# Second MLP: its first product for pairs of batches by Strassen's scheme, weights and x by way of DRAM

## Chip, cores and metric

One Trainium2 chip, one of its cores. The metric is the device time of one execution in microseconds; less is better. TensorE multiplies, VectorE and ScalarE and GpSimd do the elementwise work, SyncE (SP) issues the DMAs.

## What is computed

Attention over 4 batches x 12 heads (448 positions, 64 wide) with RMS-normalized q and k, then two MLPs over the 1792 rows:

```python
x = attn_out                       # 1792 x 768
h = ((x @ w1) * (x @ w2)) @ w3     # d_ff 1024
x = h @ w_out                      # 1792 x 768
h = x @ w_in                       # 768 x 2048   <- "first product of the second MLP"
g = h * clip(h + 3, 0, 6) / 6
out = g @ w_out2                   # 2048 x 768
```

Weights arrive as 64-bit floats. Every product is taken in three passes: each operand is split into a rounded part (hi) and the rest (lo), and hi*hi, hi*lo and lo*hi are added in one bank.

## The kernel before

Everything is kept transposed: features on the 128 partitions, the 448 positions of one batch (`S`) along the free dimension. One matmul is a 128x128 block of weights against 128x448 of data into one of 8 banks (tags `s`, `t`, `v`, `f`, two banks each).

The attention runs in steps written out by hand; between its instructions `fill` slips in the products of the first MLP (`products`: `layer1(b)`, `layer2(b)` for batches 0 to 3) and, through `prep`, their weights. The first MLP's results go to DRAM (`x2d`) for batches 0 to 2. Those of batch 3 are split straight out of the bank (`L["x2"]`), since the second MLP takes batch 3 first (`order`).

When the attention is over, a loop (L858) issues the rest of the first MLP and, every third step, converts one tile of the second MLP's weights (`conv_w`, `convert`: two passes on ScalarE L137 and L138, two on VectorE L140 and L143). The 32 converted tiles (16 of `win`, 16 of `wo2`, 128x768 each) stay in SBUF as `wf`. The second MLP is the loop L893: for each batch and each of 16 column blocks `m` it splits one tile of `win` and one of `wo2` (`split`: ScalarE copy L851, GpSimd subtraction L852), takes h in 18 matmuls (6 blocks of 128 features x 3 passes, tile `h`), applies the activation (ScalarE L930, VectorE L931), splits g (L934, L935), and takes 18 matmuls of the second product for the step before (`l4_part`, tile `acc`, six banks that collect over all 16 steps). `mm3` (L81 to L83) issues the three passes. Conversions left over are issued among the steps of the first batch. All DMAs go through SP's queue (`dma`, L88).

The order on each engine is set by a planner that takes the program's order as priority and moves ahead what it believes ready; `tc.issue_after` pins an instruction behind another.

## Time and profile before

| what | us |
|---|---|
| median of 3 runs | 1222.15 (1221.26 to 1225.3) |
| span of the profiled execution, first to last instruction | 1219.5 |
| what lies around it, against the median | 2.65 |
| TensorE busy | 1160.4 |
| VectorE, ScalarE, GpSimd busy | 756.6, 726.6, 464.9 |
| second MLP, from 738.2 to the end | 481.3 |

The profile names each group of instructions by line, engine, operation and tile. A matmul's record (0.37 us) overlaps the next one's, so the spacing of starts is what a matmul costs. The busy time of VectorE and GpSimd includes time in which an instruction has begun and is held up. The page gives no time of its own for the profiled execution other than the span.

### The profile page before, as it was taken

Reading aid. Unit: us, or ns where it says so; the run is one execution under the profiler, and the core shown is the slowest. Engines: PE = TensorE matmul, PEld = TensorE weight load, DVE = VectorE, ACT = ScalarE, POOL = GpSimd, SP = SyncE. Lnnn points to the kernel's source line nnn. Section 1 sums busy time; section 2 is a strip of 40 time slices with the busy share of each in tenths; the row PEclk is TensorE's granted clock in tenths of the full one; section 3 lists DMA queues with packets and bytes.
Section 4 is the critical chain, followed back from the end, with each engine's and each line's share of the span. In section 5 each row is a group of like instructions: output and inputs, shape, how many; then the busy total and the mean of one; then the engine's idle time right before and its main releaser. Section 6 shows DMA issues by size and latency. Waiting matters only on the chain.

```text
span 1219.5 us, 16961 instructions
## 1 busy us (share of the span) xinstructions
PE 1160.4 (95%) x5868; PEld 1020.5 (84%) x5868; DVE 756.6 (62%) x1474; ACT 726.6 (60%) x1401; POOL 464.9 (38%) x316
## 2 busy tenths in 40 slices
...
PEclk9799998999999999999999999999999999999999
...
GB/s 277 209 220 239 191 188 196 251 284 293 334 265 254 222 224 249 228 240 197 148 187 360 355 304 207 156 101 23 91 1 1 4 88 1 1 1 46 1 1 46
...
## 3 DMA queue, kind: packets, MB, share of 16 engines
...
q8 instruction: 46, 0.75, 0.3%
...
## 4 chain that ended last, share of the span: by engine, by line
PE 75%; DVE 7%; ACT 5%; DMA 5%; issue 4%; POOL 3%; SPq 0%; ACTq 0%; POOLq 0%; DVEq 0%
PE bank L340 10%; PE acc L81 7%; PE acc L83 7%; PE acc L82 6%; PE h L81 6%; PE h L82 6%; PE h L83 6%; PE bank L345 5%; PE bank L592 4%; PE bank L81 3%; PE bank L82 3%; PE bank L83 3%; DVE PP L573 2%; PE bank L566 2%; PE bank L567 2%
## 5 line engine op out<-in xcount | busy, mean ns | idle before, releaser
L852 POOL TENSOR_TENSOR wis<-wf,wis 128x768 fp32r<-128x768 f32 x63 | 120.0, 1904 | 220.0 <-ACT wis L851 219.9
L340 PE MATMUL bank<-xhl,ws 128*128 128x448 f32 x768 | 184.9, 372 | 2.5 <-ACT bs L316 2.4
L931 DVE SCALAR_TENSOR_TENSOR u<-u,h 128x448 f32<-128x448 f32 x64 | 39.5, 618 | 210.6 <-ACT u L930 210.6
L340 PEld LDWEIGHTS bank<-xhl,ws 128*128 128x128 f32 x768 | 145.1, 191 | 16.5 <-ACT bs L316 3.1
L852 POOL TENSOR_TENSOR wos<-wf,wos 128x768 fp32r<-128x768 f32 x64 | 121.4, 1896 | 91.0 <-ACT wos L851 91.0
L585 ACT ACTIVATE PP<-PP,mx 112x448 f32<-112x448 f32 x192 | 127.2, 664 | 45.0 <-DVE mx L580 36.4
L573 DVE CUSTOM_DVE_ANT_0 PP<-bank,rb,rq 112x448 f32<-112x448 f32 x192 | 129.0, 675 | 34.8 <-PE bank L567 23.9
L83 PE MATMUL acc<-g,wos 128*128 128x448 f32 x384 | 141.3, 368 | 0.0
L82 PE MATMUL acc<-g,wos 128*128 128x448 f32 x384 | 141.3, 368 | 0.0
L81 PE MATMUL acc<-g,wos 128*128 128x448 f32 x384 | 140.0, 368 | 0.0
L81 PE MATMUL h<-x2h,wis 128*128 128x448 f32 x378 | 139.2, 368 | 0.5 <-DVE u L931 0.4
L82 PE MATMUL h<-x2h,wis 128*128 128x448 f32 x378 | 138.9, 367 | 0.0
L83 PE MATMUL h<-x2h,wis 128*128 128x448 f32 x378 | 137.4, 364 | 1.3 <-POOL wis L852 1.3
L930 ACT ACTIVATE u<-h,half 128x448 f32<-128x448 f32 x64 | 40.7, 636 | 156.0 <-PE h L83 156.0
L935 DVE TENSOR_TENSOR g<-u,g 128x448 fp32r<-128x448 f32 x64 | 105.2, 1645 | 37.5 <-ACT g L934 37.5
L851 ACT ACTIVATE wos<-wf 128x768 fp32r<-128x768 f32 x64 | 54.2, 847 | 85.9 <-PE acc L83 85.7
L601 ACT ACTIVATE xh<-bank 128x448 fp32r<-128x448 f32 (+1 forms) x156 | 83.0, 539 | 32.6 <-PE bank L592 29.4
L566 PE MATMUL bank<-K,Q 128*112 128x448 f32 x192 | 76.7, 400 | 25.6 <-DVE mx L573 13.1
L611 DVE TENSOR_TENSOR xl<-bank,xh 128x448 fp32r<-128x448 f32 x142 | 87.3, 616 | 21.9 <-ACT xh L601 20.6
L592 PE MATMUL bank<-ident,PP 112*128 112x112 f32 x672 | 94.4, 264 | 6.0 <-DVE xl L611 5.2
L592 PEld LDWEIGHTS bank<-ident,PP 112*128 112x128 f32 x672 | 77.7, 142 | 26.8 <-issue 6.8
L345 PE MATMUL bank<-xhl,ws 128*128 128x448 f32 x384 | 95.4, 367 | 0.0
...
## 6 DMA issues: line engine op xcount, KB each, us to landing
...
```

The costliest lines, as they stand in the source:

```text
L81: nc.tensor.matmul(ps, lh, rh, start=first, stop=False)
L82: nc.tensor.matmul(ps, lh, rl, start=False, stop=False)
L83: return nc.tensor.matmul(ps, ll, rh, start=False, stop=last)
L340: nc.tensor.matmul(ps[:, :S], w[:, 0, ks], x[:, y, :], start=k == 0 and y == 0, stop=False)
L345: nc.tensor.matmul(ps[:, :S], w[:, 1, ks], L["xhl"][i][:, 0, :], start=False, stop=k == KD - 1)
L566: nc.tensor.matmul(ps[:CP, :S], qs, k1[:, j, :], start=True, stop=False)
L573: anchors[8 * i + s].append(nc.vector.tensor_tensor_reduce(out=T["PP", i][:, c, sl], in0=ps[:CP, :S], in1=T["rb", i][:, sl], op0=ALU.mult, ...
L585: anchors[8 * i + s].append(nc.scalar.activation(v, v, AF.Exp, bias=T["m", i][:, 8 + s : 9 + s], accum_out=T["sum", i][:, s : s + 1]))
L592: nc.tensor.transpose(ps[:, c * CP : c * CP + CP], src[:, c, kb * P : kb * P + P], ident[:CP, :CP])
L611: nc.vector.tensor_sub(lo, ps, hi)
L852: nc.gpsimd.tensor_sub(t[:, 1, :], wf[q], t[:, 0, :])
L935: nc.vector.tensor_sub(g[:, 1, :], u, g[:, 0, :])]
```

## The change

The batches are taken in pairs (0, 1) and (2, 3), and the column blocks of `win` in pairs. With the 6 feature blocks cut into two halves of 3, h of a pair of batches and a pair of column blocks is a 2x2 by 2x2 block product. It is taken in 7 block products of 3 x 3 matmuls (P1 to P7, Strassen's scheme in Winograd's form) where 8 stood. Sums of weight blocks (S1 to S4, VectorE, `prepare`) and of x blocks (T1 to T4, VectorE, `xprep`, `xrest`) are made ahead. The sums of the products are made partly by adding on in a bank (P1+P6+P7+P4 in one, P5+P3 in the other) and partly on VectorE from copies that ScalarE takes of a bank between (`snap`). Only two banks (`sA`, `sB`) serve the products; they change roles after each P4.

The second product of the pair's first batch (`L0` to `L3`) is issued between the products; that of the second batch (kind `M`) follows when all 16 column blocks are done, from g's unsplit form kept in SBUF (`G`). Splits of weights are made for half tiles of 384 columns, the subtraction in turn on VectorE and GpSimd (`halves`).

The 32 converted tiles no longer stay in SBUF: a ring of 12 buffers holds them, each is written to DRAM (`wfd`) at its first release and read back for each later use. All of x passes through `x2d`. The operands of the first pair are built once the last batch's `layer1` is issued, those 22 and T4 of it at the beginning of the second MLP, those of the second pair during the first pair's `M`. The pool of the first MLP is cut in two so that one part is freed ahead of the last `layer2`.

The core of the diff (at the last hunk the removed lines are those from L802 to L944, and the loading, indexing and output code is left out):

```diff
@@ -54,7 +55,8 @@
     rkd = dpool.tile([NP, 2 * S], F32, name="rkd")
     rsd = dpool.tile([NP, 2, S], F32, name="rsd")
     w12d = dpool.tile([M1, 2, P, 2 * DM], F32, name="w12d")
-    x2d = dpool.tile([B - 1, KD, P, S], F32, name="x2d")
+    x2d = dpool.tile([B, KD, P, S], F32, name="x2d")
+    wfd = dpool.tile([2 * M2, P, DM], F32, name="wfd")
     wpd = dpool.tile([KD * M1 // 6, P, 6, 2 * P], F32, name="wpd")
 
     cpool = ctx.enter_context(tc.tile_pool(name="consts", bufs=1, side="left"))
@@ -152,6 +154,9 @@
         yield from wprime()
         for b in range(B):
             yield from layer1(b)
+            if b == B - 1:
+                L["xm"].__exit__(None, None, None)
+                L["half"] = True
             yield from layer2(b)
 
     W = {}
@@ -260,6 +265,8 @@
     def open_l1():
         L["cm"] = tc.tile_pool(name="l1", bufs=1, side="right", **RW)
         pool = L["cm"].__enter__()
+        L["xm"] = tc.tile_pool(name="l1x", bufs=1, side="right", **RW)
+        L["xp"] = L["xm"].__enter__()
         raw, ws = defaultdict(list), {}
         L.update(ws=ws, xhl={}, abh={}, cur=0, pool=pool)
         pieces = [(u, h) for u in range(2, 2 * M1) for h in range(2)]
@@ -268,7 +275,7 @@
         def load():
             if pieces:
                 u, h = pieces.pop()
-                raw[u].append(fetch(pool, w12[u // 2, 1 - u % 2][:, h * NH : h * NH + NH], NH, "raw", 4))
+                raw[u].append(fetch(L["xp"], w12[u // 2, 1 - u % 2][:, h * NH : h * NH + NH], NH, "raw", 4))
 
         def item(u):
 
@@ -303,7 +310,7 @@
             prep[0].step()
 
     def xsplit(i):
-        d = L["pool"].tile([P, 2, S], F32R, tag="xhl", bufs=XB, name="xhl")
+        d = L["xp"].tile([P, 2, S], F32R, tag="xhl", bufs=XB, name="xhl")
         xs = xs_ready.pop(i)
         nc.scalar.activation(d[:, 0, :], xs, AF.Copy)
         nc.gpsimd.tensor_sub(d[:, 1, :], xs, d[:, 0, :])
@@ -357,12 +364,9 @@
         pool = L["pool"]
 
         def evac(n, ps):
-            if b < B - 1:
-                st = pool.tile([P, S], F32, tag="bs", bufs=2, name="bs")
-                nc.scalar.activation(st, ps[:, :S], AF.Copy)
-                dma(x2d[b, n], st)
-            else:
-                L["x2"](n, ps)
+            st = pool.tile([P, S], F32, tag="bs", bufs=2, name="bs")
+            nc.scalar.activation(st, ps[:, :S], AF.Copy)
+            dma(x2d[b, n], st)
 
         for n in range(KD):
             ps = bank("f")
@@ -799,148 +803,310 @@
-...
+    NWF, NWT, AHEAD2 = 12, 8, 6
+    PAIRS = ((0, 1), (2, 3))
...
+    uses = []
+    for p in range(2):
+        for j in range(M2 // 2):
+            uses += [("in", 2 * j), ("in", 2 * j + 1)]
+            if j:
+                uses += [("out", 2 * j - 2), ("out", 2 * j - 1)]
+        uses += [("out", M2 - 2), ("out", M2 - 1)]
+        uses += [("out", q) for q in range(M2)]
...
+    def units():
+        n = 0
+        for v, (kind, q) in enumerate(uses):
+            while v >= used[0] + NWF:
+                yield None
+            t = mp.tile([P, DM], F32, tag="wf", bufs=NWF, name="wf")
+            if v in fresh:
+                r = wr.pop(v)
+                if r.dtype == F32:
+                    nc.gpsimd.tensor_copy(t, r)
+                    yield 0.9
+                else:
+                    yield from convert(t.bitcast(I32), r)
+                n += 1
+                load_raw(n + 1)
+                yield 0.0
+            else:
+                dma(t, wfd[q + (M2 if kind == "out" else 0)])
+                yield 0.0
+            wf[v] = t
+    unit = units()
...
+    def drop(v):
+        kind, q = uses[v]
+        t = wf.pop(v)
+        used[0] += 1
+        if v in fresh:
+            dma(wfd[q + (M2 if kind == "out" else 0)], t)
...
+    def halves(t, src):
+        nc.scalar.activation(t[:, 0, :], src, AF.Copy)
+        nsplit[0] += 1
+        (nc.vector if nsplit[0] % 2 else nc.gpsimd).tensor_sub(t[:, 1, :], src, t[:, 0, :])
         return t
 
+    def xprep(p):
+        b1, b2 = PAIRS[p]
+        for k in range(KD // 2):
+            x = {}
+            for z, b, n in (("11", b1, k), ("21", b1, k + 3), ("12", b2, k), ("22", b2, k + 3)):
+                x[z] = utile()
+                dma(x[z], x2d[b, n])
+            t1, t2 = utile(), utile()
+            nc.vector.tensor_sub(t1, x["12"], x["11"])
+            nc.vector.tensor_sub(t2, x["22"], t1)
+            for z, src in (("11", x["11"]), ("21", x["21"]), ("T2", t2), ("T1", t1)):
+                xo[z, k] = halves(xtile(z, k), src)
+                yield 1.2
+            nc.vector.tensor_sub(x["12"], x["22"], x["12"])
+            xo["T3", k] = halves(xtile("T3", k), x["12"])
+            yield 1.8
+    def xrest(p):
+        x = []
+        for k in range(KD // 2):
+            x.append(utile())
+            dma(x[k], x2d[PAIRS[p][1], k + 3])
+        for k in range(KD // 2):
+            xo["22", k] = halves(xtile("22", k), x[k])
+            yield 1.2
+            d = utile()
+            nc.vector.tensor_sub(d, xo["21", k][:, 0, :], xo["T2", k][:, 0, :])
+            nc.vector.tensor_sub(x[k], xo["21", k][:, 1, :], xo["T2", k][:, 1, :])
+            nc.vector.tensor_add(d, d, x[k])
+            xo["T4", k] = halves(xtile("T4", k), d)
+            yield 1.8
+    ORDER = ("P1", "P2", "P6", "L0", "L1", "P5", "P7", "L2", "L3", "P3", "P4")
+    RIGHT = {"P1": "11", "P2": "21", "P6": "T2", "P5": "T1", "P7": "T3", "P3": "22", "P4": "T4"}
...
+    def prepare(i):
+        kind, p, j, v, h = items[i]
+        if kind[0] != "P":
+            upto(v)
+            t = mp.tile([P, 2, NH], F32R, tag="wt", bufs=NWT, name="wt")
+            wt[i] = halves(t, wf[v][:, h * NH : h * NH + NH])
+            if h:
+                drop(v)
+            return
+        upto(v[1])
+        a11, a12 = wf[v[0]][:, :NH], wf[v[0]][:, NH:]
+        a21, a22 = wf[v[1]][:, :NH], wf[v[1]][:, NH:]
+        def temp(z, x, y, op):
+            sx[z] = mp.tile([P, NH], F32, tag="sx", bufs=3, name="sx")
+            nc.vector.tensor_tensor(out=sx[z], in0=x, in1=y, op=op)
+            return sx[z]
+        if kind == "P6":
+            temp("S1", a21, a22, ALU.add)
+            temp("S2", sx["S1"], a11, ALU.subtract)
+        src = dict(P1=a11, P2=a12, P4=a22).get(kind)
+        if src is None:
+            if kind == "P7":
+                src = temp("S3", a11, a21, ALU.subtract)
+            elif kind == "P3":
+                src = temp("S4", a12, sx["S2"], ALU.subtract)
+            else:
+                src = sx["S2" if kind == "P6" else "S1"]
+        t = mp.tile([P, 2, NH], F32R, tag="wt", bufs=NWT, name="wt")
+        wt[i] = halves(t, src)
+        if h:
+            drop(v[0])
+            drop(v[1])
...
+        if now[0] % 2 and "half" not in L:
+            spend(1.5)
+        if "half" in L:
+            if xg is None:
+                xo["cm"] = tc.tile_pool(name="xl", bufs=1, side="left", **RW)
+                xo["pool", True] = d1.enter_context(xo["cm"])
+                xg = xprep(0)
+            for _ in range(2):
+                if next(xg, None) is None:
+                    prep_to(ready[0] + 1 if ready[0] < AHEAD2 else 0)
+    for _ in xg:
+        pass
...
+    def finish(p, j, z, src):
+        b, q = (z % 10 - 1), 2 * j + z // 10 - 1
+        if b == 0:
+            _, u = nonlinear(src, None)
+            gsplit(p, 0, q, u)
+            return
+        if (p, j) not in G:
+            G[p, j] = rp.tile([P, 2, S], F32, tag="G", bufs=M2 // 2, name="G")
+        nonlinear(src, G[p, j][:, q % 2])
+    sA, sB = bank("s", "sA"), bank("s", "sB")
+    swap = [(sA, sB)]
+    snap = {}
+    def product(kind, i, ps, first):
+        w = wt.pop(i)
+        z = RIGHT[kind]
+        for k in range(KD // 2):
+            ks = slice(k * P, k * P + P)
+            x = xo[z, k]
+            for n, (a, c) in enumerate(((0, 0), (0, 1), (1, 0))):
+                nc.tensor.matmul(ps[:, :S], w[:, a, ks], x[:, c, :], start=first and k == 0 and n == 0,
+                                 stop=k == KD // 2 - 1 and n == 2, skip_group_check=not first)
+    def strassen(i):
+        kind, p, j, _, _ = items[i]
+        a, c = swap[0]
+        own = c if kind in ("P2", "P5", "P3") else a
+        product(kind, i, own, kind in ("P1", "P2", "P5"))
+        r = own[:, :S]
+        if kind in ("P1", "P6", "P5"):
+            snap[kind] = utile()
+            nc.scalar.activation(snap[kind], r, AF.Copy)
+            return
+        if kind == "P4":
+            finish(p, j, 21, r)
+            swap[0] = (c, a)
+            return
+        s, z = {"P2": ("P1", 11), "P7": ("P5", 22), "P3": ("P6", 12)}[kind]
+        s = snap.pop(s)
+        nc.vector.tensor_add(s, r, s)
+        finish(p, j, z, s)
...
+    prep_to(AHEAD2)
+    xg = xrest(0)
+    for i, it in enumerate(items):
+        prep_to(i + AHEAD2)
+        kind, p, q = it[:3]
+        for _ in range(3):
+            next(xg, None)
+        if kind == "M":
+            if it[4] == 0 and q == 0:
+                for z in range(2):
+                    gsplit(p, 1, z, G[p, 0][:, z])
+                if p == 0:
+                    xg = chain(xprep(1), xrest(1))
+            if it[4] == 0 and q + 2 < M2:
+                gsplit(p, 1, q + 2, G[p, q // 2 + 1][:, q % 2])
+        spend(1.0)
+        (strassen if kind[0] == "P" else layer4)(i)
```

## Rows read from the trace of the kernel before

**Rows 1.** The page: busy time by engine, and TensorE's granted clock in 40 slices.
```profile
PE 1160.4 (95%) x5868; PEld 1020.5 (84%) x5868; DVE 756.6 (62%) x1474; ACT 726.6 (60%) x1401; POOL 464.9 (38%) x316
...
PEclk9799998999999999999999999999999999999999
```

**Rows 2.** Stretches: length; PE, PEld, DVE, ACT, POOL busy (count); clock, DMA share, GB/s.
```profile
738.20:1219.50 481.30, 475.87 (x2311) 432.95 (x2309) 216.04 (x193) 216.01 (x319) 241.08 (x127) 1.00 0.13 46
...
760.00:800.00 40.00, 40.00 (x196) 36.55 (x195) 33.99 (x29) 27.43 (x38) 22.80 (x12) 1.00 0.48 165
...
937.00:974.00 37.00, 37.00 (x182) 33.78 (x181) 15.95 (x16) 16.35 (x25) 17.98 (x11) 1.00 0.00 0
```

**Rows 3.** Waits of TensorE, 640 to 1220 us: total, times, longest.
```profile
PE h L83 <- POOL wis L852: 1.3, 2, 0.8
PE h L81 <- DVE u L931: 0.4, 1, 0.4
```

**Rows 4.** Timeline near 1200: start, duration, engine, line, operation [idle before].
```profile
1200.68 0.36 PE L83 MATMUL h<-x2h,wis 128*128 128x448 f32 x1
...
1201.14 0.64 ACT L930 ACTIVATE u<-h,half 128x448 f32<-128x448 f32 x1 [2.83 <-PE h L83]
...
1201.81 0.62 DVE L931 SCALAR_TENSOR_TENSOR u<-u,h 128x448 f32<-128x448 f32 x1 [4.31 <-ACT u L930]
...
1208.08 0.36 PE L83 MATMUL h<-x2h,wis 128*128 128x448 f32 x1
```

**Rows 5.** Groups by line and shape: busy us, mean ns | idle before.
```profile
L935 DVE TENSOR_TENSOR g<-u,g 128x448 fp32r<-128x448 f32 x64 | 105.2, 1645 | 37.5 <-ACT g L934 37.5
...
L930 ACT ACTIVATE u<-h,half 128x448 f32<-128x448 f32 x64 | 40.7, 636 | 156.0 <-PE h L83 156.0
L931 DVE SCALAR_TENSOR_TENSOR u<-u,h 128x448 f32<-128x448 f32 x64 | 39.5, 618 | 210.6 <-ACT u L930 210.6
...
L934 ACT ACTIVATE g<-u 128x448 fp32r<-128x448 f32 x64 | 37.0, 579 | 13.0 <-DVE u L931 13.0
...
L137 ACT ACTIVATE wr<-wr 128x768 f32<-128x768 f32 x29 | 26.2, 902 | 28.3 <-DMA wr<-in_win_dram 17.5 <-DMA wr<-in_wo_dram 10.8
L138 ACT ACTIVATE wr<-wr 128x768 int32<-128x768 uint16 x29 | 25.9, 894 | 0.0
...
L287 ACT ACTIVATE ws<-raw 128x384 fp32r<-128x384 f32 x28 | 15.3, 548 | 1.7 <-DVE raw L143 1.5
...
L362 ACT ACTIVATE bs<-bank 128x448 f32<-128x448 f32 x18 | 9.7, 537 | 13.6 <-PE bank L83 13.6
L224 DVE TENSOR_TENSOR wst<-bank,wst 128x384 fp32r<-128x384 f32 x16 | 8.7, 550 | 6.4 <-ACT wst L223 6.1 <-ACT xs L652 0.3
```

**Rows 6.** Timeline of VectorE and GpSimd, 756 to 767 us.
```profile
756.37 2.39 POOL L852 TENSOR_TENSOR wis<-wf,wis 128x768 fp32r<-128x768 f32 x1 [1.73 <-ACT wis L851]
...
756.97 2.60 DVE L140 SCALAR_TENSOR_TENSOR wr<-wr 128x768 int32<-128x768 int32 x1
...
762.02 0.61 DVE L935 TENSOR_TENSOR g<-u,g 128x448 fp32r<-128x448 f32 x1
762.56 0.94 DVE L140 SCALAR_TENSOR_TENSOR w<-w 128x768 int32<-128x768 int32 x1
763.54 0.96 DVE L143 SCALAR_TENSOR_TENSOR wf<-w 128x768 int32<-128x768 int32 x1
```

**Rows 7.** GpSimd subtractions, L289 and L309: duration ns minimum/median/maximum, first and last start.
```profile
L289 POOL TENSOR_TENSOR ws<-raw,ws x28: 1020/1036/2352, 232.0 to 326.8; 128x384 fp32r<-128x384 f32 x28
...
L309 POOL TENSOR_TENSOR xhl<-xs,xhl x24: 1143/1155/1554, 213.6 to 640.8; 128x448 fp32r<-128x448 f32 x24
```

**Rows 8.** Stretches of 10 us with gaps on TensorE, columns as in group 2.
```profile
190.00:200.00 10.00, 9.21 (x44) 7.80 (x44) 9.84 (x24) 5.57 (x14) 2.66 (x3) 0.71 0.52 188
200.00:210.00 10.00, 10.00 (x59) 8.98 (x58) 8.16 (x26) 9.80 (x22) 2.74 (x2) 1.00 0.78 255
210.00:220.00 10.00, 8.46 (x46) 6.37 (x45) 9.61 (x25) 9.36 (x21) 9.72 (x9) 1.00 0.83 277
```

**Rows 9.** Timeline of ScalarE, 755 to 761 us.
```profile
755.45 0.84 ACT L851 ACTIVATE wis<-wf 128x768 fp32r<-128x768 f32 x1
...
760.14 0.58 ACT L934 ACTIVATE g<-u 128x448 fp32r<-128x448 f32 x1 [1.73 <-DVE u L931]
```

199 lines of the change are left out of this document (85 added, 114 removed).

## The prediction, made before the result was known

> **What bounds the kernel now.** I read the busy times first: TensorE is busy 95% of the span and at full clock in nearly every slice after the first third [rows 1]. That share mixes stages, so I then read the stretches. From the end of the first MLP (738.2 us) to the end TensorE is busy 475.9 of 481.3 us, VectorE and ScalarE 216 each, GpSimd 241; the undisturbed stretch 937 to 974 has TensorE busy for all of its 37 us at clock 1.00 [rows 2]. The list of what TensorE waited for shows 1.7 us named waits in the last 580 us [rows 3]. So the second MLP is a queue of matmuls back to back, and its length is their number times their spacing. The spacing is not the 0.37 us of one record (records overlap): the last matmul of a step's h starts at 1200.68 and that of the next step at 1208.08, 36 matmuls later [rows 4], so 7.40/36 = 0.2056 us.
>
> **Gain.** Before, h takes 4 batches x 16 column blocks x 18 = 1152 matmuls. Afterwards a pair of batches and a pair of column blocks ("a block pair", 8 of them for each pair of batches) take 7 products of 9: 2 x 8 x 63 = 1008. The second product stays at 1152. 144 x 0.2056 = 29.6 us. The Trainium skill ("TensorE: Matmul & The Clock Gate", section "Wait — 56ns, not 53.3ns?") states N / 2.4 GHz plus about 2.5 ns between matmuls, 189 ns for 448 columns; by it the gain would be an estimated 27.2 us. The row has 206, and the row decides.
>
> Everything else the change does is to be paid for by the other engines, in a stage where TensorE has no spare time. I split it into the product phase (block pairs 0 to 7, with the second product of the first batch between them: 63 + 36 = 99 matmuls, 20.35 us each), and the M phase (second product of the second batch: 16 x 18 matmuls, 59 us), each twice.
>
> **Work of one block pair, second pair of batches.** ScalarE: 11 copies of 384 columns x 0.548, 3 copies of banks x 0.537, 4 Relu x 0.636, 2 splits x 0.579 [rows 5] = 11.3 us. VectorE: 4 Strassen sums and half of 11 subtractions, 9.5 x 0.55 = 5.2; 7 operations with a bank as operand x 0.618 = 4.3 [rows 5]; 2 splits of g x 0.61 [rows 6]; 10.8 us in all. GpSimd: 5.5 subtractions of 384 x 1.03 [rows 7] = 5.7 us. All lie well under 20.35, so TensorE remains the bound here.
>
> **The same with conversions (first pair).** The weights come as 64-bit floats; converting a tile takes two ScalarE passes of 0.90 and 0.89 [rows 5] and two VectorE passes of 0.94 and 0.96 [rows 6]. In before, 17 of 32 are finished ahead of or early in the long stage and the rest ride on a VectorE with much room. Afterwards at most 12 lie ready (the ring of 12 buffers); before had converted about 11 by the end of the last batch's first layer at the same pacing, so I take 12 to 14 before block pair 1 and 18 to 20 to do during block pairs 1 to 5, as fast as they are used, 4 to a block pair. ScalarE: 11.3 + 4 x 1.80 = 18.5 us of 20.35. VectorE: 10.8 + 4 x 1.90 = 18.4 us.
>
> That would still fit, but VectorE and GpSimd block one another. A VectorE operation that starts during a GpSimd one with all operands in SBUF ends only after it: 2.60 us for an operation that takes 0.94, begun while GpSimd was at work from 756.37 on; the split of g takes 0.61 when GpSimd idles [rows 6] and 1.65 on average [rows 5]. Operations that read a bank are not held up (0.618 mean over 64 [rows 5]). How much of GpSimd's 5.7 us is lost to VectorE? In the stretch 760 to 800 VectorE shows 34.0 us [rows 2] for 18 conversion passes (0.95) and 11 others (0.61), 23.8 us of own work: 10.2 us lost against 12 subtractions of 1.84 = 22.1 us on GpSimd, 46%, with VectorE's own load at 60%. At 90% load the share is between this and 100%: 18.4 + 0.46 x 5.7 = 21.0, or 18.4 + 5.7 = 24.1 us a block pair. So VectorE, not TensorE, sets the pace there, 0.7 to 3.8 us over 20.35. I take 2.1 (the load is nearer the upper case, but seven of its operations read banks and can run beside GpSimd). Over 4.5 block pairs: +9.5 us, bounds 3 to 17.
>
> **Two banks.** Products now alternate between two banks, and a bank is added to again or overwritten two products later, so each copy or sum out of a bank has the 9 matmuls of the product between, 1.85 us, where h before had the 18 of a second product as well. After the last matmul of a bank starts, Relu starts 0.46 us later, and the VectorE operation that reads the bank ends 1.75 us later (1202.43 for 1200.68) [rows 4]. Product P4 needs just this chain before the next block pair's P2 may overwrite its bank, which starts 10 x 0.2056 = 2.06 us after that matmul: 0.3 us to spare. The others (one copy or one sum) have about 1 us. ScalarE and VectorE are each half busy, so the chain meets an operation of some 0.6 us in its way every other time: on average 2 x 0.5 x 0.3 = 0.3 us, just the slack, with excess only in the longer cases. I take 0.3 us x 14 handovers = 4 us (0 to 12; those of the first pair overlap with the VectorE bound above).
>
> **Start.** The operands 22 and T4 of the first pair are built in space that the first MLP holds to its end; they are 9 VectorE sums, 6 splits: 12 x 0.61 + 3 x 1.15 [rows 7] = 10.8 us, besides the ordinary work, and P3 needs 22 and P4 needs T4 some 9.3 us into the stage (five products, no second product between yet). Matmuls of the first batch can be taken ahead meanwhile. +3 us (0 to 8). The waits for weights before [rows 3] lie just here and fall away: -1 (0 to -2). The copies of the other five operands lie under the 29 us of the last second layer, in which TensorE needs little of VectorE; if that cover were gone they would cost their 18 us of VectorE and GpSimd.
>
> **M phase of the first pair.** In its first 8 items (14.8 us) the operands of the second pair are issued: 18 VectorE sums and 21 splits. VectorE: (18 + 10.5) x 0.62 + 8 x 0.59 = 22.4 us; GpSimd: 10.5 x 1.15 + 4 x 1.03 = 16.2 us, of which 46 to 100% holds VectorE up: 30 to 39 us. The splits of g and weights stand behind them. The sixth split of g is issued at item 8 and wanted at item 12, 22.2 us in: 8 to 17 us late if the queue keeps the program's order. It need not: the planner reorders by readiness (the split of g of one step stands behind the split of the next step's weights on ScalarE [rows 9]), and the sums wait for x from DRAM, so that the splits can pass. +5 us (0 to 14). If g is late, the whole M phase behind it is late.
>
> **DRAM, queues.** Weights written back and read again are 384 KB a tile, 4 a block pair at most, against a stage that moves 46 GB/s on average, DMA share 0.13 [rows 2]. They are issued on SP's queue, which carries nothing else there but x, raw weights and results; a read that waits for its buffer holds up the next raw load, hidden by the 12-tile ring. Nothing, with up to 3 us if a raw load behind it comes late. The tail (last results) is unchanged.
>
> **Sum.** -29.6 + 9.5 + 4 + 3 - 1 + 5 = -9.1 us. 1219.5 - 9.1 = 1210.4 us of span; the median of the runs lies 2.65 above the span, so 1213.
>
> **Rivals.** (1) TensorE stays the bound everywhere: the planner fits sums and bank reads beside GpSimd's work, handovers cost nothing, M keeps its pace. -29.6 + 3 + 2 + 1 = -23.6: 1198.5. For it: VectorE's and ScalarE's own sums fit under 20.35 us. Against: 90% load on both, with mutual blocking. (2) The two-bank handover decides, slower: if the VectorE step of the P4 chain each time stands behind an operation held up by GpSimd (1.65 us mean for such a split [rows 5]), each handover costs 1.65 - 0.3 = 1.35 us, and 16 of them, with 5 more at the copies of P1 under the conversions, about 28 us instead of 4: +15, 1237; with half of that, 1225. It decides from about 1.2 us a handover: 14 x 1.2 = 17, against the 13 that the rest of the sum leaves. (3) The terms meet their upper middle (VectorE 13, handover 7, start 5, M 8): -29.6 + 33 - 1 = +2, 1224, no change that counts.
> (4) The clock falls. Where TensorE was broken up, its clock fell to 0.71 at 190 to 200 us, yet stayed at 1.00 at 210 to 220 with TensorE busy 8.46 of 10 [rows 8]. The Trainium skill (same page, "Why this matters for your kernels") says that idle gaps between bursts bring the lower of the two levels (1.2 instead of 2.4 GHz); the rows agree, but show that many short gaps need not. If one 10 us stretch in each of the first eight block pairs ran at 0.75, that is 8 x 2.5 = 20 us: 1233.
>
> **How the numbers follow.** Forecast (1205 to 1218) 0.38; rival 1 (below 1205) 0.18; rival 3 (within 0.3%, 1218.5 to 1225.8, about what a measurement of this kernel can tell from no change) 0.17; slower 0.27, of it the handover 0.17, the M phase or VectorE at their upper ends 0.06, the clock 0.04. Faster 0.56, same 0.17, slower 0.27. The range from 1198 to 1236 leaves out about 2 in 10. The forecast's own range is 1205 to 1218.
>
> **What would show it.** Right: 1008 product matmuls at 0.206 us; VectorE busy over 95% from about 760 to 860 us, with TensorE at 88 to 92% there and waiting for VectorE; TensorE near 100% in the second pair's block pairs, its few waits at the first matmul of P2; a dip early in the first M phase. Wrong: TensorE over 97% while weights are converted (then rival 1), waits of over 1 us at every P2 or P6 in the second pair too (rival 2), the clock under 0.95 in the stage (rival 4).

## The result, and the profile after

| what | before | after |
|---|---|---|
| median of 6 runs each, us | 1221.70 (1219.58 to 1225.3) | 1230.95 (1230.61 to 1236.88) |
| ratio, with its 95% interval | | 1.0076 [1.0052, 1.01] |
| profiled execution: time, span, mean granted clock | span 1219.5, clock 0.985 | 1232.8, 1231.0, clock 0.976 |
| matmuls | 5868 | 5724 |

The kernel became slower by 0.76%, 9.3 us; the forecast was 1213 us, faster. It lies inside the range (1198 to 1236).

Lines of the changed kernel that the rows name: L139 and L140 (ScalarE), L142 and L145 (VectorE) convert a raw tile `wr` into `wf`; L882 and L884 split an operand (copy, subtraction); L960 makes sums of weight blocks; L1059 copies a bank, L1067 adds a bank to such a copy; L1014 and L1015 are Relu and product of the activation; L1022 and L1023 split g. L1048 is a matmul of a block product (banks `sA`, `sB`), L83 to L85 are those of the second product (`acc`); L347 and L323 belong to the first MLP. `wt`, `xo` and `g` are the split operands.

From the page of after (it answers [rows 1]): span, busy times, TensorE and its granted clock in 40 slices of 30.8 us.

```profile
span 1231.0 us, 17457 instructions
...
PE 1140.3 (93%) x5724; PEld 999.5 (81%) x5724; DVE 861.1 (70%) x1739; ACT 771.9 (63%) x1585; POOL 390.0 (32%) x329
...
PE   3699988899999999999999997799999899999998
...
PEclk9699998899999999999999998999999999999999
```

TensorE's busy time fell by 20.1 us (from 1160.4), not by the 29.6 of 144 matmuls, and its idle time rose by 31.6 (1231.0 - 1140.3 = 90.7, before 59.1). The two make the 11.5 us of the span. Of the missing 9.5 us of busy time some 6 are matmuls at the slower clock (36 of them after 640 us follow each other at about 0.37 in place of 0.206 us); the rest stands at the edges of the stops, where the record of the last matmul (0.37 us) is not overlapped by a next one. Two slices at 0.7 (738 to 800 us) and one at 0.8 (954 to 985) show where.

Stretches of the second MLP of after (answer to [rows 2]); columns: length, then busy us (and instructions) of TensorE, its weight loads, VectorE, ScalarE, GpSimd, then granted clock, DMA share, GB/s:

```profile
740.00:760.00 20.00, 14.22 (x64) 11.59 (x62) 17.91 (x21) 12.57 (x23) 8.65 (x7) 0.92 0.73 234
760.00:780.00 20.00, 14.95 (x60) 12.41 (x61) 19.16 (x27) 12.66 (x21) 9.65 (x5) 0.91 0.64 193
780.00:800.00 20.00, 16.71 (x82) 15.00 (x81) 15.26 (x22) 13.44 (x25) 4.66 (x4) 1.00 0.58 187
800.00:820.00 20.00, 19.95 (x98) 18.00 (x96) 15.34 (x21) 12.99 (x24) 5.96 (x5) 1.00 0.45 124
820.00:840.00 20.00, 15.24 (x65) 13.28 (x66) 15.46 (x24) 13.29 (x23) 4.87 (x4) 0.91 0.72 232
840.00:860.00 20.00, 19.59 (x96) 17.73 (x95) 17.35 (x23) 13.15 (x24) 5.72 (x5) 1.00 0.77 233
...
960.00:980.00 20.00, 13.92 (x61) 12.11 (x60) 20.00 (x31) 10.12 (x23) 8.85 (x6) 0.91 0.35 105
...
1000.00:1160.00 160.00, 160.00 (x784) 146.86 (x782) 88.16 (x143) 82.83 (x159) 44.25 (x43) 1.00 0.29 89
```

The second pair's product phase (1000 to 1160) has no gap: TensorE is busy for all 160 us. The loss lies in the first pair, up to its M phase, and ahead of the second M phase. From 760 to 860 TensorE is busy 86.4 us of 100, VectorE 82.6. Only from 760 to 780 and from 960 to 980 is VectorE full or nearly so.

What TensorE waited for in after, 640 to 1231 us (answer to [rows 3]); columns: us in total, times, longest:

```profile
PE acc L84 <- DVE g L1023: 8.0, 3, 4.0
PE acc L83 <- ACT g L1022: 6.6, 4, 2.5
PE sA L1048 <- DVE u L1015: 6.3, 3, 2.5
PE sB L1048 <- DVE u L1015: 3.7, 2, 3.3
PE sB L1048 <- ACT u L1059: 2.4, 1, 2.4
PE sA L1048 <- POOL xo L884: 2.1, 1, 2.1
```

Before had 1.7 us of waits here; after has 32. To place them I took from TensorE's timeline the distance between the starts of neighbouring matmuls beyond 0.2056 us; this counts a wait and the slow matmuls behind it together (the first spacing behind a stop, 0.31 us, is left out: 0.1 us each, some 2 us in all). "Lost" below always means this:

| stretch of after, us | lost, us |
|---|---|
| 740 to 780, start and first block pairs | 14.5 |
| 780 to 905, block pairs with conversions | 13.7 |
| 932, ahead of the first M phase | 2.2 |
| 945 to 1005, M phase of the first pair | 7.7 |
| 1005 to 1160, second pair | 0 |
| 1162, ahead of the second M phase | 3.7 |

Together 41.8 us, where before lost 2.4 (all between 742 and 750 us). -29.6 + 41.8 - 2.4 = +9.8. In addition the last `layer1` begins 2.6 us later in the profiled execution of after (654.25 against 651.64); some 1 us the other way is not traced.

Five of these waits, those for `u` of L1015 (10.0 us together), stand at one place: the first matmul of P2 in block pairs 1 to 5, which may overwrite its bank only when the activation of the last P4 has read it.

### The profile page after: what moved, and what is told of

It reads as the page before. It is cut to its first block, busy times and chain, and to the rows that moved or that the text cites. A ratio compares the mean times of both kernels' runs of the same rounds, so it can differ in the third digit from the quotient of the medians.

```text
span 1231.0 us, 17457 instructions
## 1 busy us (share of the span) xinstructions
PE 1140.3 (93%) x5724; PEld 999.5 (81%) x5724; DVE 861.1 (70%) x1739; ACT 771.9 (63%) x1585; POOL 390.0 (32%) x329
## 4 chain that ended last, share of the span: by engine, by line
PE 62%; DVE 13%; DMA 11%; ACT 7%; issue 5%; POOL 2%; SPq 1%; DVEq 0%; ACTq 0%; POOLq 0%
PE bank L347 9%; PE sB L1048 7%; PE sA L1048 6%; PE acc L84 5%; PE acc L83 5%; PE acc L85 5%; PE bank L352 5%; PE bank L596 4%; DMA wr<-in_win_dram 3%; PE bank L84 3%; PE bank L83 3%; PE bank L85 3%; PE bank L570 2%; PE bank L571 2%; PE bank L649 2%
## 5 line engine op out<-in xcount | busy, mean ns | idle before, releaser
L347 PE MATMUL bank<-xhl,ws 128*128 128x448 f32 x768 | 185.3, 372 | 0.3 <-DVE bs L326 0.2
L884 POOL TENSOR_TENSOR wt<-wf,wt 128x384 fp32r<-128x384 f32 x91 | 102.7, 1133 | 223.4 <-ACT wt L882 217.2
L347 PEld LDWEIGHTS bank<-xhl,ws 128*128 128x128 f32 x768 | 145.5, 191 | 14.9 <-ACT ws L294 1.3
L84 PE MATMUL acc<-g,wt 128*128 128x448 f32 x384 | 143.5, 374 | 8.0 <-DVE g L1023 8.0
L85 PE MATMUL acc<-g,wt 128*128 128x448 f32 x384 | 137.9, 372 | 0.0
L83 PE MATMUL acc<-g,wt 128*128 128x448 f32 x384 | 128.5, 373 | 6.6 <-ACT g L1022 6.6
L882 ACT ACTIVATE wt<-wf 128x384 fp32r<-128x384 f32 x176 | 89.9, 519 | 59.5 <-PE acc L85 40.6
L1048 PE MATMUL sA<-xo,wt 128*128 128x448 f32 x504 | 114.4, 369 | 11.0 <-DVE u L1015 6.3
L1048 PE MATMUL sB<-xo,wt 128*128 128x448 f32 x504 | 114.0, 369 | 6.3 <-DVE u L1015 3.7
L1048 PEld LDWEIGHTS sA<-xo,wt 128*128 128x128 f32 x504 | 94.9, 189 | 21.7 <-DVE u L1015 7.4
L1048 PEld LDWEIGHTS sB<-xo,wt 128*128 128x128 f32 x504 | 94.8, 189 | 16.2 <-DVE u L1015 4.5
L605 ACT ACTIVATE xh<-bank 128x448 fp32r<-128x448 f32 (+1 forms) x156 | 82.9, 539 | 31.2 <-PE bank L596 28.2
L615 DVE TENSOR_TENSOR xl<-bank,xh 128x448 fp32r<-128x448 f32 x142 | 87.4, 617 | 21.5 <-ACT xh L605 20.1
L84 PEld LDWEIGHTS acc<-g,wt 128*128 128x128 f32 x384 | 73.8, 192 | 16.0 <-DVE g L1023 9.4
L884 DVE TENSOR_TENSOR wt<-wf,wt 128x384 fp32r<-128x384 f32 x85 | 55.6, 654 | 42.7 <-ACT wt L882 42.5
L83 PEld LDWEIGHTS acc<-g,wt 128*128 128x128 f32 x384 | 72.8, 190 | 14.4 <-ACT g L1022 8.1
```

Source lines behind the costliest of these rows:

```text
L83: nc.tensor.matmul(ps, lh, rh, start=first, stop=False)
L84: nc.tensor.matmul(ps, lh, rl, start=False, stop=False)
L85: return nc.tensor.matmul(ps, ll, rh, start=False, stop=last)
L347: nc.tensor.matmul(ps[:, :S], w[:, 0, ks], x[:, y, :], start=k == 0 and y == 0, stop=False)
L882: nc.scalar.activation(t[:, 0, :], src, AF.Copy)
L884: (nc.vector if nsplit[0] % 2 else nc.gpsimd).tensor_sub(t[:, 1, :], src, t[:, 0, :])
```

## Experiments

Each was timed beside runs of the kernel before (medians 1221.5 to 1224.5 us over the sets); a gain or loss is against the changed kernel's 1230.95 us unless another kernel is named. The diffs show the lines that make the change; lines that only carry it through are left out. Line numbers shift by a few lines where an edit adds some.

### The wait ahead of each M phase (932 and 1162 us)

Theory: the first M item waits for the split of its g, issued late. The edit issues the two splits some items earlier (`e1_split_early`).

```diff
+        if kind == "L" and q == M2 - 2 and it[4] == 0:
+            for z in range(2):
+                gsplit(p, 1, z, G[p, 0][:, z])
         if kind == "M":
-            if it[4] == 0 and q == 0:
-                for z in range(2):
-                    gsplit(p, 1, z, G[p, 0][:, z])
-                if p == 0:
-                    xg = chain(xprep(1), xrest(1))
+            if it[4] == 0 and q == 0 and p == 0:
+                xg = chain(xprep(1), xrest(1))
```

> Edit: the first two splits of g for the second batch of a pair are issued four items earlier. In the changed kernel TensorE stops for 2.16 us before the first matmul of each M phase (932 and 1162 us) and then runs about 9 matmuls at 0.37 instead of 0.206 us. Theory (the split is issued too late, nothing else is missing): both stops and both slow stretches go, 2 x (2.2 + 1.5) = -7 us, 1224. Rival (VectorE or ScalarE is behind in its order there anyway): the stop stays or moves by one item, 0 to -2 us.

1230.85 us, ratio to before 1.0083 [1.0064, 1.0102]; both waits stood unchanged (2.15 us lost at 930.96 and at 1161.99). The theory fell. The matmuls behind the wait read another g, that of block 15, which comes out of the last P4: the planner had moved the second product of block 14 ahead of that P4, so nothing was left to cover block 15's Relu, VectorE product and split. `e7_last` pins block 14's second product behind the last product's last matmul.

```diff
-        (strassen if kind[0] == "P" else layer4)(i)
+        with tc.issue_after(lastmm[0].ins) if kind == "L" and q == M2 - 2 else ExitStack():
+            (strassen if kind[0] == "P" else layer4)(i)
```

> Edit: on TensorE the second product of column block 14 is pinned behind the last P4 of each pair. In the changed kernel the planner takes it ahead of that P4, so that block 15 follows P4 at once and waits 2.16 us for Relu, activation and split (931 and 1162 us), and e1_split_early, which issued other splits earlier, kept this wait at 2.16 us. Theory: 18 matmuls, 3.7 us, then cover that chain; both stops go with the slow stretch behind them, 2 x (2.2 + 0.8) = -6 us, 1225. Rival (block 14's own operand is late): the stop moves ahead of block 14, 0 to -2 us.

1227.56 us (1222.77 to 1232.31, 10 runs), ratio 1.0049 [1.003, 1.0068]: 3.4 us less, and both waits are gone: the cause is shown. Less is gained than the 5.9 us that stood there; in its trace the conversions and the first M phase lose 1.7 us more than in after.

### The second pair's x operands in the first M phase

The changed kernel takes three steps of building x operands with each item. `e2_x_slow` takes one step with each M item; `e6_x_slow_own` does so too and lets VectorE and GpSimd take turns for x and for weights separately, since in e2 the shared turn gave every weight subtraction to GpSimd (a stop of 7.1 us at 972.48, for a weight from GpSimd).

```diff
-        for _ in range(3):
+        for _ in range(1 if kind == "M" else 3):
             next(xg, None)
```

> Edit: during the M phase of the first pair one step of building the second pair's x operands is issued per item instead of three. The changed kernel stops for 2.2 and 4.2 us at 963 and 971 us on the split of g and then runs about 9 matmuls slowly. Theory (sums and splits of x stand ahead of g's splits in VectorE's order and are held up by GpSimd): the stops go, -6 to -8 us, 1223 to 1225. Rival (they wait for x from DRAM and would stop wherever they are issued): the stops move later in the M phase or to the start of the second pair, 0 to -2 us.

> Edit: one step of the second pair's x operands per item of the M phase, as in e2_x_slow, but splits of x and of weights alternate between VectorE and GpSimd each for themselves. In e2_x_slow one split of each kind fell on every item, so that all weight splits of the stretch went to GpSimd (9 in a row, 2.4 us each, where 1.0 is its own time) and TensorE waited 7.0 us for them. Theory (the x operands need only be spread, the engine assignment did the harm): the stops of 8 us in e2's and 6.4 us in the changed kernel's first M phase go, 1222 to 1225. Rival (any x work in the M phase holds g up): a stop of over 3 us remains, 1227 to 1231.

e2: 1233.0 us, ratio 1.0094 [1.0074, 1.0113]; e6: 1230.76, 1.0073 [1.0044, 1.0101]. Both theories missed. In e6's M phase the waits for g shrank to 1.0 us, but this took their place (TensorE's waits, 905 to 1231 us):

```profile
PE acc L85 <- POOL wt L884: 4.2, 1, 4.2
```

`f3_nox` leaves the whole building out:

```diff
                 if p == 0:
-                    xg = chain(xprep(1), xrest(1))
+                    xg = iter(())
```

> Leaves out the building of the second pair's x operands (loads, sums and splits); the second pair multiplies those of the first, so batches 2 and 3 come out with other values. It measures the whole cost of that work in the M phase of the first pair: the two stops for a g split at 963 and 971 us (2.07 and 4.01 us) and the slow-clock matmuls behind them should go, 6 to 8 us, to 1223 to 1225. If the stops stay at half their length or more, it is the adds and splits of M alone that VectorE can't keep up with, and the time falls by 0 to 3 us.

1223.08 us, ratio 1.001 [0.9992, 1.0027]: 7.9 us less, and in the first pair's M phase nothing is lost any more. So the work costs what was read off, 8 us; spreading it did not help, since then a weight was late from GpSimd. It costs this only beside GpSimd: `f4_vector` below has all of this work and more on VectorE, and loses nothing there.

### The conversion of the weights in the first pair

`e3_noconv` leaves out the conversion: the tiles of the ring are read as float32 from DRAM (other data, the same size).

```diff
-                    yield from convert(t.bitcast(I32), r)
+                dma(t, r)
```

> Edit: no weight of the second MLP is converted; each tile is instead read as 384 KB of float32 that the first MLP left in DRAM (the numbers are other ones, so what is computed is not the second MLP's product). Theory A (conversions are the cause of the stops between 745 and 875 us: their passes stand ahead of bank reads in the order of ScalarE and VectorE): about 14 of the 28 us of stops from 745 on go, and all of the 13.6 us after 795; -14 to -22 us, 1209 to 1217. Theory B (the sums and splits for Strassen's scheme alone overload VectorE together with GpSimd): under -6 us.

1217.09 us (10 runs), ratio 0.996 [0.9947, 0.9974]: 13.9 us less; lost from 740 to 905 us are 4.1 instead of 28.2. So the conversion in the first pair is the largest single cost. The time tells less of it than the stretch, as the edit has a cost of its own: from 640 to 740 us, where after loses 0.4, e3 loses 8.3 us, most of it in waits for loads from the DRAM tensor that its tiles are read from too (`w12d`).

```profile
PE bank L347 <- DMA ws<-w12d: 5.4, 3, 3.3
```

Two theories of how followed from this piece of after, the timelines of ScalarE, VectorE, SP and TensorE:

```profile
817.27 0.62 ACT L1014 ACTIVATE u<-sA,half 128x448 f32<-128x448 f32 x1
...
823.00 0.89 ACT L139 ACTIVATE wr<-wr 128x768 f32<-128x768 f32 x1 [4.70 <-DMA wr<-in_wo_dram]
823.79 0.56 ACT L1022 ACTIVATE g<-u 128x448 fp32r<-128x448 f32 x1
...
817.86 1.36 DVE L960 TENSOR_TENSOR sx<-wf,sx 128x384 f32<-128x384 f32 x1
819.15 0.55 DVE L884 TENSOR_TENSOR wt<-sx,wt 128x384 fp32r<-128x384 f32 x1
819.62 0.61 DVE L1015 SCALAR_TENSOR_TENSOR G<-u 128x448 f32<-128x448 f32 x1
820.15 0.95 DVE L145 SCALAR_TENSOR_TENSOR wf<-wr 128x768 int32<-128x768 int32 x1
821.02 0.55 DVE L960 TENSOR_TENSOR sx<-wf 128x384 f32<-128x384 f32 x1
821.49 0.61 DVE L1015 SCALAR_TENSOR_TENSOR u<-u,sA 128x448 f32<-128x448 f32 x1
...
818.01 0.33 SPq L91 DMA_DIRECT2D wr<-in_wo_dram  x1
...
822.15 1.08 PE L1048 MATMUL sA<-xo,wt 128*128 128x448 f32 x4 [2.21 <-DVE u L1015]
```

The raw load issued at 818.01 is there at 823.00, 5 us later, and ScalarE stands before it for 4.70 us with a split of g (L1022) queued behind. The long stop of TensorE here has another end: Relu was done at 817.9, but L1015 ran on VectorE only at 821.49, behind five operations, one of them a conversion pass (L145) and one drawn out to 1.36 us. Of the four longest stops from 780 to 905 us two are of this kind (822 and 871 us), and ahead of the other two (799 and 834 us) ScalarE waits 1.89 and 1.36 us for a raw load. Theory A1: these waits (23 us between 738 and 885) are the cost. Theory A2: the passes' own time on VectorE and ScalarE is. `f1_noload` takes all loads but the first two away and keeps the passes; `f2_onepass` keeps the loads and takes both VectorE passes and one of the two on ScalarE away.

```diff
-        if n < len(fresh):
-            kind, q = uses[fresh[n]]
-            wr[fresh[n]] = fetch(...)
+        if 2 <= n < len(fresh):
+            wr[fresh[n]] = wr0[n % 2]
+        elif n < 2:
+            kind, q = uses[fresh[n]]
+            wr0[n] = wr[fresh[n]] = fetch(...)
```

> Leaves out the loads of all raw weights but the first two: every conversion pass stays and reads those two buffers again and again, so the weights that are made are not the real ones. It parts two theories of the roughly 14 us that the version without any conversion gave back (1217.1 against 1231.0 us). Theory A1, the wait: a conversion's first pass on ScalarE waits 2 to 5 us for a raw load, and ScalarE holds up the g splits and Relus queued behind it, on which TensorE waits; then without the loads the time falls by 8 to 14 us, to 1217 to 1223, and ScalarE's waits for loads between 738 and 885 us (23 us in the changed kernel) are gone. Theory A2, the passes themselves: the time that VectorE and ScalarE spend on them is what is missing; then the time falls by 0 to 3 us, to 1228 to 1231, though the waits are gone.

```diff
-                    yield from convert(t.bitcast(I32), r)
+                    nc.scalar.activation(t, r[:, :, 1].bitcast(F32), AF.Copy)
+                    yield 2.5
```

> Keeps every raw load and its wait, but makes each weight in one pass on ScalarE out of the high words alone, in place of the passes on ScalarE and VectorE (leaves out the rounding to 11 bits and the exponent, so the weights are not the real ones). The mirror of the run without loads: by A2 (the passes' own time) the time falls by 10 to 14 us, to 1217 to 1221; by A1 (the wait for a load in ScalarE's order) it falls by 0 to 4 us, to 1227 to 1231.

f1: 1215.53 us (1209.61 to 1222.76, 10 runs), ratio 0.9957 [0.9935, 0.9978], 15.4 less. f2: 1209.52, ratio 0.9902 [0.9877, 0.9927], 21.4 less. Each gains more than its own theory had allowed, but f2 does not part the two: from 738 to 885 us ScalarE waits for no raw load in f2 either, where after has 23 us of it. With a shorter conversion a buffer is free sooner and the next load is issued sooner (argued, not shown). By stretch, 740 to 905 us, after loses 28.2 us, f1 some 10 (the traced execution is its fastest), f2 7, e3 4.1. So without the loads and the waits for them, with every pass still there, about two thirds of the loss is gone; the passes alone cost some 6 us. The gains of f1 and f2 are no two shares of a sum: the conversion is a chain (load, two ScalarE passes, two VectorE passes, buffer free, next load) on engines that also serve TensorE, and both edits take the same wait out of it.

Two tries to take only the waiting away failed. `e4_raw4` has four raw buffers for two, paid for with four of the ring's twelve; `e5_pin` pins the conversion's ScalarE passes behind the last weight split.

```diff
-    NWF, NWT, AHEAD2 = 12, 8, 6
+    NWF, NWT, AHEAD2, NWR = 8, 8, 6, 4
-                load_raw(n + 1)
+                load_raw(n + NWR - 1)
```

> Edit: four buffers for raw weights instead of two, eight converted tiles instead of twelve (same space), every load issued two conversions earlier. Theory A1 (the conversions' harm is their wait for the raw load, 4.9 us a tile, with ScalarE standing at the first pass): ScalarE's waits for raw tiles from 738 to 880 us fall from 23 us to under 8, and the time by 8 to 14 us, 1217 to 1223. Theory A2 (it is the passes' own 7.6 us of VectorE a block pair and the mutual blocking with GpSimd): 0 to -4 us though the waits for raw tiles fall.

```diff
     def spend(us):
-        while us > 0:
+        with tc.issue_after(lastact[0].ins) if lastact[0] else ExitStack():
+            while us > 0:
```

> Edit: in the second MLP each piece of a conversion is pinned behind the weight split issued last on ScalarE; nothing is left out. In the changed kernel ScalarE stands 23 us at the first conversion pass for the raw load (738 to 885 us, up to 4.7 us at a time), and with four raw buffers it stood 20 us, each time until 4.9 us after the load was issued: the planner moves the pass up to where it believes the load landed. Theory A1 (it is this wait, in ScalarE's order, ahead of copies of banks and splits of g): the waits for raw tiles fall below 10 us and the time by 6 to 14 us, 1217 to 1225. Theory A2 (the passes' own time on VectorE): the waits may fall, the time by under 3 us.

e4: 1240.49 us, ratio 1.0156 [1.0139, 1.0172], 9.5 more. ScalarE still waited 20 us for raw loads, and the first MLP lost 10.2 us from 640 to 740, where after loses 0.4. TensorE's waits of e4 there:

```profile
PE bank L347 <- ACT bs L323: 4.9, 1, 4.9
PE bank L347 <- DMA ws<-w12d: 2.2, 3, 0.8
```

The longest one is for a copy of the first MLP (`bs`) that stood on ScalarE behind a weight split, which waited 4.27 us for its weight sum (L960) on VectorE, behind conversion passes now taken earlier. The others are loads of the first MLP, at a DMA share of 1.02 from 660 to 720 us (0.98 to 1.02 in after too).

e5: 1229.95 us, ratio 1.007 [1.0048, 1.0091]; the waits stayed (25 us), so it says nothing on A1. `e8_all` joins e5, e6 and e7:

> Edits of e5_pin, e6_x_slow_own and e7_last together. If each theory holds and they are independent: -10 (e5) - 7 (e6) - 6 (e7) = -23 us, 1208, faster than the kernel before by 1%. If only the M-phase and last-block edits hold: -13, 1218.

1223.85 us, ratio 1.0008 [0.9986, 1.0029]: level with before; from 740 to 905 us it still loses 28.0.

### The subtractions on GpSimd

`f4_vector` gives GpSimd's half of the split subtractions to VectorE.

```diff
-        (nc.vector if nsplit[0] % 2 else nc.gpsimd).tensor_sub(t[:, 1, :], src, t[:, 0, :])
+        nc.vector.tensor_sub(t[:, 1, :], src, t[:, 0, :])
```

> All second-half subtractions of the operand splits go to VectorE; GpSimd has none of them. Theory of mutual blocking (VectorE and GpSimd hold each other up, an operation of 0.55 to 0.61 us taking 1.4 to 1.6 us beside GpSimd's): VectorE then loses no more time to GpSimd than it gains work, and the time stays within 3 us of 1231 or falls by up to 6. Theory of load (VectorE simply has too much to do in the first pair's product phase, and what is moved there comes on top): a block pair of the first pair grows from about 18.4 us of VectorE's own work to about 21.4, TensorE waits for it through the first five block pairs, and the time rises by 6 to 15 us, to 1237 to 1246.

1213.67 us, ratio 0.9939 [0.9917, 0.9961]: 17.3 us less, far beyond what either theory had expected, and faster than before. The gain lies in two places: from 740 to 905 us some 18 us are lost in place of 28.2, and in the first M phase nothing in place of 7.7, though VectorE is nearly as full there: 36.0 us from 940 to 980, where after has 37.3. The second half of that, in f4 (the row of after stands above):

```profile
960.00:980.00 20.00, 20.00 (x102) 18.77 (x101) 15.96 (x31) 8.98 (x18) 0.00 (x0) 1.00 0.39 119
```

ScalarE's waits for raw loads are still 22 us there, so GpSimd is a second cause in the first pair beside them. VectorE's groups by form, 740 to 880 us, columns: busy us, mean ns, idle before. First after, then f4:

```profile
L145 DVE SCALAR_TENSOR_TENSOR wf<-wr 128x768 int32<-128x768 int32 x21 | 25.9, 1232 | 0.1
L142 DVE SCALAR_TENSOR_TENSOR wr<-wr 128x768 int32<-128x768 int32 x20 | 19.2, 961 | 17.7 <-ACT wr L140 17.6
L884 DVE TENSOR_TENSOR wt<-wf,wt 128x384 fp32r<-128x384 f32 x18 | 12.7, 707 | 2.1 <-ACT wt L882 2.1
L884 DVE TENSOR_TENSOR wt<-sx,wt 128x384 fp32r<-128x384 f32 x10 | 7.5, 751 | 0.0
L960 DVE TENSOR_TENSOR sx<-wf,sx 128x384 f32<-128x384 f32 x5 | 5.3, 1066 | 0.0
L1067 DVE TENSOR_TENSOR u<-sA,u 128x448 f32<-128x448 f32 x8 | 4.9, 617 | 0.4 <-ACT g L1022 0.3
L884 DVE TENSOR_TENSOR xo<-u,xo 128x448 fp32r<-128x448 f32 x5 | 4.9, 997 | 0.0
```

```profile
L884 DVE TENSOR_TENSOR wt<-wf,wt 128x384 fp32r<-128x384 f32 x41 | 22.3, 552 | 3.1 <-ACT wt L882 3.1
L142 DVE SCALAR_TENSOR_TENSOR wr<-wr 128x768 int32<-128x768 int32 x20 | 19.2, 958 | 11.5 <-ACT wr L140 11.3
L145 DVE SCALAR_TENSOR_TENSOR wf<-wr 128x768 int32<-128x768 int32 x20 | 19.1, 953 | 0.0
L884 DVE TENSOR_TENSOR wt<-sx,wt 128x384 fp32r<-128x384 f32 x24 | 13.3, 552 | 2.1 <-ACT wt L882 2.1
L884 DVE TENSOR_TENSOR xo<-u,xo 128x448 fp32r<-128x448 f32 x9 | 5.3, 620 | 0.0
L960 DVE TENSOR_TENSOR sx<-wf,sx 128x384 f32<-128x384 f32 x6 | 3.3, 552 | 0.0
```

In f4 every operation takes 0.55, 0.62 or 0.96 us by its size; in after the same ones take up to twice as long in the mean. Two rows do not: the sum that reads a bank (L1067, 617 ns) and the first conversion pass (L142, 961 against 958), though both of its operands lie in SBUF. Of the nine L142 that met a GpSimd subtraction seven had begun before it. Against f4's means the rows shown lose 21 x 0.279 + 18 x 0.155 + 10 x 0.199 + 5 x 0.514 + 5 x 0.377 = 15.1 us, and all groups of the stretch 20, while GpSimd worked for 45 us (8.65 + 9.65 + 4.66 + 5.96 + 4.87 + 5.72 + 5.54 in stretches of 20): 0.45 us lost for each. In that time GpSimd made 35 subtractions, which VectorE would have made in 35 x 0.56 = 20 us. The help saved VectorE nothing. The Trainium skill ("Perfetto Trace Analysis", section "Optimizing Scalar/DVE Operations") says just this, that moving operations between these two "might not help", as they share a port to SBUF; the rows put a number to it, 0 saved of 20 us. It shows in VectorE's total from 740 to 880 us too: busy 114.9 us of these 140 in after, 118.0 in f4, which got further by then.

Whether the hold-up costs, or the later results of GpSimd, is told apart by `g3_vector_idle`: VectorE does all that counts, and GpSimd works beside it for nobody.

```diff
+        if nsplit[0] % 2 == 0:
+            o = mp.tile([P, 320], F32R, tag="idle", bufs=1, name="idle")
+            nc.gpsimd.tensor_sub(o, t[:, 0, :320], t[:, 0, :320])
```

> All subtractions that count on VectorE, and GpSimd makes, as often as in the changed kernel and after the same ScalarE passes, subtractions of 128x320 whose result nobody reads. Hold-up theory (VectorE's instructions last longer beside GpSimd's): VectorE has about 22 us more work of its own from 740 to 880 us than in the changed kernel, and again loses 0.45 us for each microsecond that GpSimd works (measured there: 20 us lost in 45), so the time goes back to that of the changed kernel or beyond, 1228 to 1245. Latency theory (what costs is that someone waits for GpSimd's results): nobody waits here, and the time stays at 1212 to 1218.

1229.96 us, ratio 1.0052 [1.0028, 1.0075]: back where the changed kernel was. VectorE in the same stretch:

```profile
L884 DVE TENSOR_TENSOR wt<-wf,wt 128x384 fp32r<-128x384 f32 x37 | 25.5, 690 | 2.9 <-ACT wt L882 2.9
L884 DVE TENSOR_TENSOR xo<-u,xo 128x448 fp32r<-128x448 f32 x11 | 9.1, 850 | 0.0
```

The hold-up theory holds: 16 us for work whose result nobody reads. The Trainium skill ("SBUF — State Buffer", section "Who interferes with whom") states that a VectorE instruction with two SBUF operands and a GpSimd one that reads SBUF exclude each other for their whole length. The trace agrees as to which forms are held up: those with both operands in SBUF, and not L1067; the pass that is L142 here was held up in the kernel before (2.60 us, [rows 6]). The share is lower than I had expected, some 14 us lost for 43 of GpSimd's, 0.33. Two reservations: that GpSimd's later results cost nothing besides is not shown (in e6 one cost 4.2 us), and a weight buffer is free only when GpSimd has read it too, so a part (perhaps the 3.5 us wait of TensorE for a ScalarE weight split in M) may be a wait for GpSimd after all.

`g1_before_vector` makes the same exchange in the kernel before (L852).

```diff
-        nc.gpsimd.tensor_sub(t[:, 1, :], wf[q], t[:, 0, :])
+        nc.vector.tensor_sub(t[:, 1, :], wf[q], t[:, 0, :])
```

> The kernel before, with the subtraction of its weight splits in the second MLP (line 852) on VectorE in place of GpSimd: the same exchange that made the changed kernel 17 us faster. If that gain belongs to the change (before, TensorE has about 1.7 us of waits after 640 us, so there is nothing to take away), the time stays within 4 us of 1222. If the exchange is good for any kernel of this kind, the time falls by 5 us or more; VectorE gets 128 subtractions of about 1 us, and g subtractions that last 0.6 in place of 1.6 us.

1220.54 us, ratio 0.998 [0.9966, 0.9995], 2.3 us less than the kernel before. Its VectorE groups, 738 to 1219 us (the second answers the g split of [rows 5]):

```profile
L852 DVE TENSOR_TENSOR wos<-wf,wos 128x768 fp32r<-128x768 f32 x64 | 61.3, 957 | 83.1 <-ACT wos L851 82.4
...
L935 DVE TENSOR_TENSOR g<-u,g 128x448 fp32r<-128x448 f32 x64 | 39.6, 618 | 1.3 <-ACT g L934 1.3
```

The split of g falls from 1645 to 618 ns, and almost nothing follows, as TensorE had next to no waits there to lose (1.7 us, now 1.5). The hold-up was in the kernel before too, for free; the change made it cost.

### What the change is worth without these costs

`g2_vector_last` is f4 with e7's pin; `g4_vector_raw3` has a third raw buffer in addition (two of the ring's twelve for it); `h1_vector_onepass` is g2 with f2's single pass.

> The changed kernel with all subtractions on VectorE, and block 14's second product pinned behind the last P4 (each of the two edits has been measured alone: 1213.7 us and 3.4 us below the changed kernel). If their gains add, 1210 us (1208 to 1212), and the two stops of 2.0 us ahead of the M phases are gone. If the wait moves to the next product, 1213 to 1214.

> The version with all subtractions on VectorE and block 14's second product pinned, with three buffers for raw weights in place of two, and 10 for made weights in place of 12, so that a raw load is issued one conversion earlier. If ScalarE's waits for raw loads (22 us between 738 and 885 us in the version with all on VectorE) still hold up the snapshots and Relus behind them, the stops at 792, 815, 836 and 858 us (together 6.4 us) go, and the time is 1202 to 1207. If the planner puts the passes forward with the loads, as with four buffers, the waits stay and the time is 1209 to 1216, more if the loads collide with those of the first MLP's weights.

> The version with all subtractions on VectorE and block 14's second product pinned, and each raw weight made in one ScalarE pass out of its high words (leaves out the rounding and the exponent, so the weights are not the real ones). If the remaining gaps come of the conversion, those from 780 to 905 us (6.7 us) go and part of those from 740 to 780, and the time is 1199 to 1203, near the 1198.5 us of TensorE alone as the bound. If they come of the two banks and of building the operands, it stays at 1206 to 1210.

g2: 1208.97 us, ratio 0.9887 [0.986, 0.9915]. The gains add (17.3 + 3.4 = 20.7 against 22.0), and this is a version of the changed kernel that does the whole computation and beats both kernels, before by 1.1%. g4: 1210.23, 0.9887 [0.9855, 0.9918], no further gain; ScalarE's waits for raw loads stayed at 20 us, and as in e4 the first MLP lost some 5 us. h1: 1194.45, 0.9751 [0.9717, 0.9785]; its stretches and all that TensorE waited for from 640 us on:

```profile
740.00:780.00 40.00, 38.50 (x183) 33.63 (x183) 30.05 (x57) 26.75 (x49) 0.00 (x0) 1.00 0.61 208
780.00:880.00 100.00, 100.00 (x491) 92.02 (x490) 63.33 (x120) 60.03 (x113) 0.00 (x0) 1.00 0.52 170
880.00:1000.00 120.00, 120.00 (x586) 109.92 (x585) 87.89 (x166) 67.68 (x135) 0.00 (x0) 1.00 0.46 144
```

```profile
PE sB L1051 <- ACT u L1063: 1.2, 1, 1.2
PE bank L347 <- DMA ws<-w12d: 0.6, 1, 0.6
PE sA L1051 <- DVE xo L885: 0.2, 1, 0.2
```

That is 30.1 us under the before of its own set (1224.54; 26 to 35 by the interval, and the two profiled spans differ by 26.6), and 4.6 us below the range that I had given: as far as the spread tells, the 29.6 of the 144 matmuls. The comparison leaves the conversion out of h1 and not out of before. Between h1 and g2 lie 14.5 us, the price that the full conversion still has when GpSimd holds nobody up.

## Why the prediction was wrong

**Gain, -29.6: right.** 144 matmuls fewer on the page, the second pair without a gap, and 30.1 us (26 to 35) in h1.

**Two banks, +4 (0 to 12): nothing where nothing is converted, and not a term by itself where something is.** TensorE is busy for all of 1000 to 1160 us, through the seven handovers of the second pair, and in h1 for all of 780 to 1160. There "an operation in the way every other time" did not happen, or the slack of 0.3 us was enough; which of them I did not measure. But in the first pair the handovers from P4 to P2 are where TensorE waits for L1015: five times, 2.0 us in the mean, longest 3.3, a third of all its waits; without conversion (e3) none of them is left. So the place was named rightly, and what stands in the way is a conversion pass or a wait for its load as well as GpSimd's hold-up: in f4 P2 still waits at all five. Rival 2 as it was written (its half case, 14 us, adds up to 1223, not 1225), with a price at every handover of both pairs, falls by its own sign, though its time (1237) lies near the result. Whether a third bank would cover the delay was not tried; the other six serve `acc`.

**Conversions, +9.5 (3 to 17), and start, +3 (0 to 8): this is the step that failed.** Together 12.5 forecast, 28.2 lost (14.5 up to 780 us, above its bound, and 13.7 behind). The start alone was about right: without conversion it loses 4.1 us in e3 and 2.5 in h1. But the sum let conversions begin with block pair 1 and none fall into the start (four ran between 740 and 770 us), where VectorE is fullest (19.16 of 20 us). And the method was wrong: it added up VectorE's time for a block pair and compared it with TensorE's 20.35 us, as if an engine with 10 or 15% to spare could not stop another. VectorE was not over 95% busy from 760 to 860, as I had said, but 82.6%, and TensorE still lost more. In f4 VectorE is busier in that stretch (86.6 us) and TensorE loses less. What stopped TensorE was a late instruction, a copy or a product of the activation behind a conversion's link in an engine's order, on ScalarE (which stood 23 us for raw loads) as well as on VectorE. One reading in it was wrong too: of the seven operations said to read a bank and to run beside GpSimd only four do; the product of the activation reads a bank after P4 alone, and otherwise a sum in SBUF. The share lost to GpSimd, 46% from [rows 2, 6], was measured right (0.45). I used it to size a load, and did not ask whether the subtractions were worth giving to GpSimd at that price; f4 answers that, 17 us, of which some 10 lie here and nearly 8 in the M phase.

**M phase, +5 (0 to 14): 7.7.** Cause and place as told (sums and splits of x ahead of the split of g, drawn out by GpSimd), the size within its bounds; f3 gives 7.9, and f4 loses nothing there with the same work.

**DRAM and queues, 0 (up to 3): wrong as a zero.** I looked at bytes and at SP's queue. The cost is the 5 us from issue to landing with two buffers, for which ScalarE waits; f1 gives 15.4 us back without the loads (part of the 28.2 above, not beside them). The clause "if a raw load behind it comes late" named the event, but bounded it with the 12-tile ring, which lies behind ScalarE, not ahead of it.

**Waits before, -1: -2.4.** **Not foreseen: +5.9** ahead of the two M phases, since the planner takes block 14's second product ahead of the last P4 (e7, 3.4 us in the medians).

**Clock (rival 4).** The granted clock did fall behind stops, to 0.91 or 0.92 in the 20 us stretches from 740, 760, 820 and 960 us, but not behind every one: it stayed at 1.00 in those from 780, 860 and 920 us, with waits of 3.3, 2.5 and 2.0 us. Behind the stop that ends at 971.47 eight matmuls follow at 0.37 us each, 1.3 us more than at full clock. In all it costs some 6 us, contained in the terms above, where the rival had 20 beside them.

By its own terms: -29.6 + 28.2 + 7.7 + 5.9 - 2.4 = +9.8 against -9.1. Of the 18.9 us between them 15.7 are the conversions and the start, 5.9 the planner's order, 2.7 M, and -4 the banks (the rest is the wait term); the waits at the handovers of the first pair are booked with the conversions, in whose stretch they lie.
